# Shifting the start addresses of one group of SBUF tiles (the gated values' parts, and what lies behind them) by 64 and 32 bytes

## The chip, the cores and the metric

The kernel runs on one core of a Trainium2 chip. The metric is the device time of one execution in microseconds. Three executions of the kernel before gave 940.1, 940.12 and 941.05 us, so the median is 940.12 us. Bytes are counted along one of the 128 partitions of SBUF, and the **offset** of a tile is its first byte modulo 256.

## The reference

Masked attention over 8 batches with 8 heads, 576 positions and a head dimension of 64; then, on the 8 × 576 = 4608 tokens with 512 channels, a gated layer of width 1536.

```python
def _attn_ref(q, k, v) -> np.ndarray:
    ...
    scores = scale * np.matmul(q, k.transpose(0, 1, 3, 2))
    mask_local = (rel >= 0) & (rel < stride)
    mask_strided = (rel >= 0) & (pos[None, :] % stride == pos[:, None] % stride)
    ...
    return np.matmul(attn, v).astype(np.float32)

def _moe_ref(x, w_gate, w_val, w_out) -> np.ndarray:
    gate = 1.0 / (1.0 + np.exp(-(x @ w_gate)))
    val = x @ w_val
    return (gate * val @ w_out).astype(np.float32)
```

## The kernel before

**Blocks.** The tokens form nine blocks of 512: block k (0 to 7) holds the first 512 positions of batch k, and block 8 the last 64 positions of all batches. Attention goes batch by batch in four pairs of heads, two with the local mask and two with the strided one. The gated layer goes through 12 slices f of 128 hidden channels each.

**Two parts for each factor.** Matrix products are made of fp32r operands, and each factor is split in two: an upper part (the value rounded to fp32r) and a lower part (the rest). A product is the sum of upper × upper, upper × lower and lower × upper, so every 128x512 product is three matmuls. The inputs' parts are `xh` and `xl`, the weights' parts lie in `w`, and the **parts of the gated value** gate · val are `hh` (upper) and `hl` (lower).

**The gated layer of a block.** Blocks 0, 1 and 2 make gate and value in `products` (L511 to L516): the weights are the stationary operand (128x128), the inputs `xh`, `xl` the moving one (128x512). Blocks 3 to 8 are made two at a time by a scheme with seven products in place of eight (L764 to L780): the products `p` and `d` have weights from a `ring` of tiles as the stationary operand and sums of inputs, `xs`, as the moving one. In all nine blocks `split_high_h` (L534, on ScalarE) rounds the gated value into `hh`, `split_low_h` (L538, on VectorE) writes the rest into `hl`, and `out_products` (L544) multiplies by the output weights: there `hh` or `hl`, 128 columns of it, is the **stationary** operand and the weights `w` the moving one. That makes 9 blocks × 12 slices × 4 pieces × 3 = 1296 matmuls with `hh` or `hl` as the stationary operand. Block 1 makes its gates and values with 12 × 2 × 12 = 288 matmuls, which read `xh1` and `xl1` as the **moving** operand.

**Order.** A table of step names, `ORDER`, is written out by hand; each engine runs its instructions in that order. The first `x` step (upper part of block 0, slice 0) comes some 60 steps ahead of block 0's first output products, while attention of batch 0 is still going.

**Where tiles lie.** Three pools follow each other in SBUF: `keep` (from byte 1152), `work` (from 140,800), and at the end `first`, which is closed when batch 0's second pair is done and gives its room to `odd`. Inside a pool a tag gets its place when it is first used, behind those used before it. `hh` and `hl` have three buffers each and are the last tags of `work`, so what follows in SBUF is only `first`, then `odd`. `first` holds the tiles of batch 0's second pair of heads (its inputs `qk`, `vv` come by DMA). `odd` holds block 1's inputs `xh1`, `xl1`; in the same two places later the plain inputs `xraw` of blocks 3 to 8; and `ost`, from which half of the results and some of the weights' sums are written out. The pad at the end of `cst` (L184) brings the tiles behind it to offset 0:

```python
    wide = SL * KL + GS + P
    cst = pool.tile([P, wide + -(wide + SPARE) % 64], F32, name="cst")[:, :wide]
```

In the kernel before every tile behind `cst` begins at offset 0, and the 128-column pieces of a stationary operand, at multiples of 512 bytes, do so too. `cst` itself begins at offset 128.

Of the kernel before, what the change touches and what calls it, by code (L numbers as in the profile page):

```python
# [9 lines left out]
F32 = mybir.dt.float32  # L10
F32R = mybir.dt.float32r
# [9 lines left out]
P = 128  # L21
# [18 lines left out]
TB = 512  # L40
# [137 lines left out]
def attention_then_glu(ctx, tc, qk_l, qk_s, v_l, v_s, w_all, consts, out):  # L178
    nc = tc.nc
    pool = ctx.enter_context(tc.tile_pool(name="keep", bufs=1))  # L180
    work = ctx.enter_context(tc.tile_pool(name="work", bufs=1))
# [327 lines left out]
    hs = {}  # L509
# [6 lines left out]
            nc.tensor.matmul(o, w, x, start=first and n == 0, stop=last and n == len(todo) - 1)  # L516

    def parts_tiles(k, f):
        hs[k, f] = [work.tile([P, TB], F32R, tag=n, name=f"{n}{k}_{f}", bufs=3) for n in ("hh", "hl")]
        return hs[k, f]  # L520

    def sigmoid(k, f, g):
# [11 lines left out]
    def split_high_h(k, f, by=nc.scalar.copy):  # L534
        hh, _ = parts_tiles(k, f)
        by(hh, whole_h[k, f])  # L536
# [409 lines left out]
```

## Time and profile before

| what | value |
|---|---|
| times of three executions | 940.1, 940.12, 941.05 us; median 940.12 |
| the profiled execution | 940.61 us, of which 938.8 us are the span of its instructions |
| VectorE, ScalarE, GpSimd busy | 604.3, 430.1, 118.1 us |
| waits of TensorE's matmuls that the trace lists | 15.0 us in all, the longest 4.8 us |
| transfers | 154.14 MB, 164 GB/s over the span |

The span runs from the first to the last instruction of the profiled execution. A matmul's row has the time from its start to the modelled end of its last column, 389 ns for a 128x512 one; as they are pipelined, the **pace** (from one start to the next) is shorter, and it is the pace that the engine's time consists of. PE is TensorE's matmul, PEld its loads of stationary operands, which go on beside the matmul ahead; DVE is VectorE, ACT ScalarE, POOL GpSimd, SP the engine that issues most DMAs.

### The profile page before, as it was taken

The page shows a single profiled execution, that of the slowest core. Times are in us where ns is not written, and L with a number is a line of the kernel's source. Part 1 is how long each engine was busy: PE and PEld are TensorE (multiplying, and loading weights), DVE is VectorE, ACT ScalarE, POOL GpSimd, SP SyncE. Part 2 cuts the span into 40 slices and gives each one's busy share as a digit, 9 for nine tenths or more (in the row PEclk, how much of TensorE's full clock was granted, in tenths as well). Part 3 has the DMA queues.
Part 4 walks back from the last instruction along what each step waited for, and adds up shares of the span by engine and source line. Part 5 has one row for each costly group of instructions (what it writes and reads, how often), then busy time and mean ns, then how long its engine had stood idle before and what let it go on. Part 6 is the DMA issues. An engine that isn't in the chain of part 4 may idle for free.

```text
span 938.8 us, 18515 instructions
## 1 busy us (share of the span) xinstructions
PE 919.2 (98%) x7624; PEld 757.2 (81%) x7624; DVE 604.3 (64%) x991; ACT 430.1 (46%) x783; POOL 118.1 (13%) x182
## 2 busy tenths in 40 slices
PE   5999999999999999999999999999999999999998
PEld 4788887888887878888888888888888888888886
DVE  6899766666688998666767897766347433333331
ACT  3899763434364555444445534443434233332221
POOL 0000002544525531000000120000002100000000
PEclk9999999999999999999999999999999999999999
DMA  9773553664656755665555434654444045444111
GB/s 360 264 243 96 166 169 117 190 184 140 201 170 191 226 188 179 212 205 166 179 188 176 156 104 151 213 186 144 146 157 137 21 158 185 150 153 143 64 46 45
DMA packets 90068, 154.14 MB, mean 164 GB/s; under 512 B 5888, under 2 KB 40192, under 8 KB 89984
## 3 DMA queue, kind: packets, MB, share of 16 engines
q1 hardware_dynamic: 89504, 152.31, 50.3%
q8 instruction: 60, 0.98, 0.4%
q10 hardware_dynamic: 480, 0.66, 0.3%
q14 instruction: 24, 0.20, 0.1%
HBM read 121.48 MB, written 31.46 MB: 163 GB/s over the span
## 4 chain that ended last, share of the span: by engine, by line
PE 91%; DVE 4%; DMA 2%; POOL 1%; ACT 1%; issue 1%; SPq 1%; DVEq 0%
PE p L774 21%; PE o L547 19%; PE d L774 16%; PE g L516 9%; PE v L516 8%; PE o_a L547 5%; PE o_g L547 3%; PE o_v L547 3%; PE x_a L437 2%; PE x L437 1%; PE s_g L333 1%; DMA k<-in_qk_s 1%; PE s_v L333 1%; PE s L333 1%; DVE pt L405 1%; PE t L392 1%
## 5 line engine op out<-in xcount | busy, mean ns | idle before, releaser
L774 PE MATMUL p<-xs,ring 128*128 128x512 f32 x864 | 204.6, 389 | 0.0
L774 PEld LDWEIGHTS p<-xs,ring 128*128 128x128 f32 x864 | 162.2, 188 | 33.7
L547 PE MATMUL o<-w,hh 128*128 128x512 f32 x576 | 180.5, 395 | 0.0
L774 PE MATMUL d<-xs,ring 128*128 128x512 f32 x648 | 155.7, 389 | 0.0
L774 PEld LDWEIGHTS d<-xs,ring 128*128 128x128 f32 x648 | 121.6, 188 | 25.3
L547 PEld LDWEIGHTS o<-w,hh 128*128 128x128 f32 x576 | 106.1, 188 | 22.8
L547 PE MATMUL o<-w,hl 128*128 128x512 f32 x288 | 112.1, 389 | 0.0
L808 DVE TENSOR_TENSOR e<-e,d 128x512 f32<-128x512 f32 x54 | 37.1, 687 | 109.2 <-PE d L774 62.1
L405 DVE STREAM_TRANSPOSE pt<-sb 32x320 f32<-32x320 f32 (+1 forms) x192 | 102.9, 536 | 3.8
L516 PE MATMUL g<-xh,w 128*128 128x512 f32 x256 | 86.7, 396 | 2.6 <-DVE sb L353 1.2
L516 PE MATMUL v<-xh,w 128*128 128x512 f32 x256 | 85.4, 391 | 0.0
L803 ACT COPY e<-p 128x512 f32<-128x512 f32 x54 | 31.7, 587 | 117.0 <-PE p L774 116.9
L547 PEld LDWEIGHTS o<-w,hl 128*128 128x128 f32 x288 | 54.1, 188 | 11.5
L516 PEld LDWEIGHTS g<-xh,w 128*128 128x128 f32 x256 | 48.3, 189 | 14.0 <-DVE sb L353 1.8
L516 PEld LDWEIGHTS v<-xh,w 128*128 128x128 f32 x256 | 48.1, 188 | 10.2
L702 POOL TENSOR_TENSOR sum<-sum 128x128 f32<-128x128 f32 x96 | 51.6, 541 | 6.4
L516 PE MATMUL g<-xl,w 128*128 128x512 f32 x128 | 50.1, 392 | 0.0
L540 DVE TENSOR_TENSOR hl<-hid,hh 128x512 fp32r<-128x512 f32 x36 | 28.0, 780 | 34.4 <-ACT hh L536 34.1
L516 PE MATMUL v<-xl,w 128*128 128x512 f32 x128 | 49.8, 389 | 0.0
L816 ACT ACTIVATE e<-e 128x512 f32<-128x512 f32 x54 | 34.2, 633 | 28.7 <-DVE e L808 28.4
L697 POOL TENSOR_TENSOR sum<-w 128x256 f32<-128x256 f32 x44 | 32.5, 759 | 105.3 <-DMA sets<-sum 62.1
L536 ACT CAST hh<-hid 128x512 fp32r<-128x512 f32 x36 | 22.4, 622 | 50.0 <-PE o_a L547 41.2
(140 smaller groups left out, 1381.3 us busy)
## 6 DMA issues: line engine op xcount, KB each, us to landing
ring<-sets SPq DMA_DIRECT2D x126, 512.0 KB, 4.0
raw<-in_w_all SPq DMA_DIRECT2D x36, 512.0 KB, 5.2
vv<-in_v_l SPq DMA_DIRECT2D x15, 640.0 KB, 4.8
qk<-in_qk_s SPq DMA_DIRECT2D x15, 599.0 KB, 5.7
qk<-in_qk_l SPq DMA_DIRECT2D x15, 592.0 KB, 5.0
out<-ob SPq DMA_DIRECT2D x32, 256.0 KB, 2.0
sets<-w SPq DMA_DIRECT2D x24, 256.0 KB, 3.9
sets<-sumh SPq DMA_DIRECT2D x24, 256.0 KB, 2.5
```

The lines of the kernel that those rows point to most:

```text
L333: nc.tensor.matmul(sc[j % len(sc)][g * m : (g + 1) * m, j // len(sc) * BANK + s * kk : j // len(sc) * BANK + (s + 1) * kk], q_[d, at : at ...
L405: nc.vector.transpose(dst[to : to + LB, :, col : col + LB], src[part * LB : (part + 1) * LB, :, h * LB : (h + 1) * LB])
L437: nc.tensor.matmul(at_bank(r, (u * per + g) * m, (u * per + g + 1) * m)[j * D : (j + 1) * D], v[part][rows, slot * P + j * D : slot * P + ...
L516: nc.tensor.matmul(o, w, x, start=first and n == 0, stop=last and n == len(todo) - 1)
L540: by.tensor_tensor(hl, whole_h.pop((k, f)), hh.bitcast(F32), op=ALU.subtract)
L547: nc.tensor.matmul(acc[k][i], h[:, i * P : (i + 1) * P], w, start=f == 0 and n == 0, stop=f == NF - 1 and n == 2,)
L697: nc.gpsimd.tensor_tensor(u[:, at : at + 2], part(wh[f][i], c), part(wl[f][i], c), op=ALU.add)
L702: nc.gpsimd.tensor_tensor(u[:, to], u[:, x], u[:, y], op=op)
L774: nc.tensor.matmul(to, w[:, (wi * 2 + c) * P : (wi * 2 + c + 1) * P], x[xi][:, c], start=p in (1, 2, 5) and c == j == 0, stop=c == 1 and j ...
L803: nc.scalar.copy(x, two[m, 0])
L808: nc.vector.tensor_tensor(x, x, two[m, 1], op=ALU.add)
L816: nc.scalar.activation(x, x, AF.Sigmoid)
```

## The change

When the parts' tiles are asked for the first time (block 0, slice 0), a small tile is placed ahead of each of the two tags, and a memset on GpSimd writes it once:

```diff
     def parts_tiles(k, f):
-        hs[k, f] = [work.tile([P, TB], F32R, tag=n, name=f"{n}{k}_{f}", bufs=3) for n in ("hh", "hl")]
+        hs[k, f] = []
+        for n, ahead in (("hh", 16), ("hl", 56)):
+            if (k, f) == (0, 0):
+                nc.gpsimd.memset(work.tile([P, ahead], F32, tag="gap" + n, name="gap" + n), 0.0)
+            hs[k, f].append(work.tile([P, TB], F32R, tag=n, name=f"{n}{k}_{f}", bufs=3))
         return hs[k, f]
```

The tiles ahead have 64 and 224 bytes. In the two built programs the tiles begin here:

| tiles | byte before | byte now | offset before | offset now |
|---|---|---|---|---|
| all of `keep`, and of `work` ahead of the parts | | the same | 0 | 0 |
| `hh`, first buffer (others 2048 and 4096 further) | 198,144 | 198,208 | 0 | 64 |
| `hl`, first buffer (the same) | 204,288 | 204,576 | 0 | 32 |
| `xh1`, `xraw` (and `sb` of batch 0's second pair) | 210,432 | 210,720 | 0 | 32 |
| `xl1`, `xraw` | 218,624 | 218,912 | 0 | 32 |
| `qk`, `vv` of batch 0's second pair | 213,760, 218,624 | 214,048, 218,912 | 0 | 32 |
| `ost` | 226,816 | 227,104 | 0 | 32 |

The weights `w`, the `ring`, `xs`, and the inputs of blocks 0 and 2 stay at offset 0. So the output products have a stationary operand at offset 64 or 32 against a moving one at 0, block 1's products a stationary one at 0 against a moving one at 32, and all other products both at 0 as before.

On PE, DVE, ACT and SP the instructions, their order and their waits are the same as before. On POOL two are new. This is POOL's program at its start before, from its first memset for the attention (`sb` of batch 0, pairs 1 and 3) to its first sums of weights:

```order
L314 MEMSET sb0_1_81 128x12x10
L314 MEMSET sb0_3_84 128x12x10
L314 MEMSET sb1_1_689 128x12x10
L314 MEMSET sb1_3_1364 128x12x10
L697 ISA
```

And this is the same place now, where the two tiles ahead of the parts have the names gaphh and gaphl:

```order
L314 MEMSET sb0_1_81 128x12x10
L314 MEMSET sb0_3_84 128x12x10
L522 MEMSET gaphh_677 128x16
L522 MEMSET gaphl_680 128x56
L314 MEMSET sb1_1_693 128x12x10
```

The two memsets stand between those of batch 0 and the first of batch 1; they wait for nothing, and nothing waits for them but the memsets behind them on POOL.

## The prediction

> **What bounds the kernel now.** I read the page's head first, then its chain of waits, then stretches of the timeline.
>
> ```profile
> span 938.8 us, 18515 instructions
> PE 919.2 (98%) x7624; PEld 757.2 (81%) x7624; DVE 604.3 (64%) x991; ACT 430.1 (46%) x783; POOL 118.1 (13%) x182
> PE 91%; DVE 4%; DMA 2%; POOL 1%; ACT 1%; issue 1%; SPq 1%; DVEq 0%
> ```
>
> TensorE has 98% of the span and 91% of the chain that ended last. A table of stretches shows how little else there is:
>
> ```profile
> core 0: us, PE busy (x) PEld busy (x) DVE busy (x) ACT busy (x) POOL busy (x), PEclk, DMA share, GB/s
> 0.00:35.00 35.00, 23.62 (x600) 19.58 (x601) 24.76 (x46) 16.02 (x37) 0.54 (x6) 1.00 0.91 341
> 360.00:540.00 180.00, 180.00 (x1586) 148.72 (x1585) 128.96 (x211) 85.32 (x156) 6.40 (x8) 1.00 0.58 185
> 735.00:905.00 170.00, 170.00 (x752) 140.77 (x751) 57.50 (x85) 50.35 (x85) 0.00 (x0) 1.00 0.39 122
> ```
>
> Only the first 35 us have real gaps (11.4 us). From 360 to 540 us and from 735 to 905 us TensorE is busy in every microsecond. So in most of the kernel the time is the number of matmuls times their **pace**, and the change leaves the number as it is. The pace is read from a piece of the chain that holds output products alone:
>
> ```profile
> 714.04 8.16 PE o L547 x36
> 893.55 8.16 PE o L547 x36
> ```
>
> 8.16 / 36 = 0.2267 us, in both stretches. The groups by shape show which matmuls the change can touch:
>
> ```profile
> L774 PE MATMUL p<-xs,ring 128*128 128x512 f32 x864 | 204.6, 389 | 0.0
> L547 PE MATMUL o<-w,hh 128*128 128x512 f32 x576 | 180.5, 395 | 0.0
> L774 PE MATMUL d<-xs,ring 128*128 128x512 f32 x648 | 155.7, 389 | 0.0
> L547 PE MATMUL o<-w,hl 128*128 128x512 f32 x288 | 112.1, 389 | 0.0
> ...
> L547 PE MATMUL o_a<-w,hh 128*128 128x512 f32 x144 | 44.3, 389 | 0.0
> L547 PE MATMUL o_a<-w,hl 128*128 128x512 f32 x72 | 28.0, 389 | 0.0
> L547 PE MATMUL o_g<-w,hh 128*128 128x512 f32 x72 | 22.4, 392 | 0.0
> L547 PE MATMUL o_v<-w,hh 128*128 128x512 f32 x72 | 22.2, 389 | 0.0
> ...
> L547 PE MATMUL o_g<-w,hl 128*128 128x512 f32 x36 | 14.0, 389 | 0.0
> L547 PE MATMUL o_v<-w,hl 128*128 128x512 f32 x36 | 14.0, 389 | 0.0
> ```
>
> The rows of L547 add up to 576 + 288 + 144 + 72 + 72 + 72 + 36 + 36 = 1296 matmuls with `hh` or `hl` as the stationary operand. With block 1's 288 (the moving operand shifts) 1584 matmuls have a shifted operand; the 1512 of L774 have none. One nanosecond of pace on the 1584 is 1.6 us, and 0.2% of the time is 1.9 us, about the least that a measurement of this kernel can tell from no change: a change of pace by 0.0012 us would be seen.
>
> **The change, part by part.**
>
> *The two memsets.* POOL's rows at the start of the timeline:
>
> ```profile
> 0.73 0.34 POOL L314 MEMSET sb<- 128x120 f32 x2 [0.29 <-POOLq L934]
> 45.07 0.21 POOL L314 MEMSET sb<- 128x120 f32 x1 [44.01 <-PE t L396]
> ```
>
> Both stand between these two, where POOL sits idle for 44.01 us. Each writes 16 or 56 columns, fewer than the 120 that take 0.21 us. Cost: at most 0.4 us inside a 44 us hole, so 0. Without that cover they would delay a memset that attention of batch 1 needs, by the same 0.4 us.
>
> *The loads of stationary operands.* A load begins with the matmul ahead of it and goes on beside it:
>
> ```profile
> L547 PEld LDWEIGHTS o<-w,hh 128*128 128x128 f32 x576 | 106.1, 188 | 22.8
> ```
>
> 188 ns of load in a pace of 227 ns leave 22.8 us / 576 = 40 ns. A load from offset 64 or 32 that takes up to a fifth longer stays hidden, if the load's own length is all that matters. I take 0.
>
> *The pace with an operand off 0.* This is the one unknown. No 128x512 matmul of the trace has its operands at different offsets, so it must be bounded. The nearest rows are the strided scores, whose operands walk through SBUF in steps of 216 bytes:
>
> ```profile
> 218.99 0.22 PE L333 MATMUL s_v<-qk 64*64 64x54 f32 x1
> ...
> 219.05 0.22 PE L333 MATMUL s_v<-qk 64*64 64x54 f32 x1
> ...
> 219.11 0.22 PE L333 MATMUL s_v<-qk 64*64 64x54 f32 x1
> ...
> 219.17 0.22 PE L333 MATMUL s_v<-qk 64*64 64x54 f32 x1
> ...
> 219.23 0.22 PE L333 MATMUL s_v<-qk 64*64 64x54 f32 x1
> ```
>
> Each of these rows opens a step of four matmuls; the stationary operand begins at offsets 16, 232, 192 and 152 in the four steps from 219.05 on (and 56 in the one ahead), the moving one 112 bytes further round. Each step takes 0.06 us whatever its offsets. These matmuls are small and may be held back by something else, so that is a sign and no proof. A second sign: `p`, `d`, `o` and `o_a` take 389 ns in the mean, or a little more behind attention, although their tiles lie at many places from 5,632 to 210,000 bytes; what matters can at most be the address below 512. Upper bound of the pace: the slowest start-to-start that the trace shows without a wait, right behind the attention's small matmuls, where load and stream have not yet fallen into step:
>
> ```profile
> 76.78 0.50 PE L516 MATMUL v<-xh,w 128*128 128x512 f32 x1
> 77.12 0.40 PE L516 MATMUL v<-xl,w 128*128 128x512 f32 x1
> 77.36 0.63 PE L516 MATMUL v<-xh,w 128*128 128x512 f32 x2
> ...
> 79.67 0.39 PE L547 MATMUL o<-w,hh 128*128 128x512 f32 x1
> ```
>
> 77.12 to 77.36 is 0.240 us, 0.0133 over the pace: 1584 × 0.0133 = +21 us. Lower bound: at the start TensorE runs at about half its pace (four transposes from 14.69 to 15.73, against 99.78 to 100.31 later: 1.04 / 0.53 = 1.96), and there a 128x512 matmul takes 0.43 us:
>
> ```profile
> 14.69 1.11 PE L392 MATMUL t<-cst,sb 128*128 128x128 f32 x4
> 15.73 0.42 PE L396 MATMUL t<-cst,sb 64*64 64x64 f32 x2
> ...
> 31.79 0.63 PE L516 MATMUL g<-xl,w 128*128 128x512 f32 x1
> 32.22 0.63 PE L516 MATMUL g<-xh,w 128*128 128x512 f32 x1
> ...
> 99.78 0.60 PE L392 MATMUL t<-cst,sb 128*128 128x128 f32 x4
> 100.31 0.30 PE L396 MATMUL t<-cst,sb 64*64 64x64 f32 x2
> ```
>
> 0.43 / 1.96 = 0.219 us; with the rounding, 0.218. So up to 0.0087 us of the full pace are something that half pace hides, and if the shift removed it all: 1584 × 0.0087 = −13.8 us. Between −13.8 and +21 I take 0, since the nearest rows (the scores) show no dependence on the offset.
>
> The Trainium skill, "TensorE: Matmul & The Clock Gate", section "Back-to-back issue gap", gives a matmul of 512 columns 512/2.4 + 2.5 = 215.8 ns from start to start; this trace disagrees, with 226.7. If equal offsets were what costs the 10.9 ns, an estimate by that page's figure is 1584 × 0.0109 = 17.3 us less.
>
> *Writers and readers of the shifted tiles on other engines.*
>
> ```profile
> L540 DVE TENSOR_TENSOR hl<-h,hh 128x512 fp32r<-128x512 f32 x36 | 24.8, 689 | 13.8 <-ACT hh L536 13.8
> L808 DVE TENSOR_TENSOR hid<-hid,d 128x512 f32<-128x512 f32 x36 | 24.8, 688 | 13.2 <-ACT hid L803 12.1
> ```
>
> VectorE needs 689 ns with both inputs in SBUF at offset 0, and 688 with one in PSUM: equal offsets cost it nothing that a shift could give back. If a shift made VectorE, ScalarE or GpSimd slower by a tenth on these tiles, the work stays in stretches in which TensorE is busy throughout (180.00 of 180.00 us above). I take 0; what would come late if that cover went is the next slice's output products, by 0.07 us a slice, 108 slices: 7.5 us.
>
> *Transfers into and out of shifted tiles.* Batch 0's second pair loads its inputs into tiles at offset 32, in the stretch where the queue bounds the start:
>
> ```profile
> q<-in_qk_l SPq DMA_DIRECT2D x1, 288.0 KB, 5.1
> ...
> cst<-in_consts SPq DMA_DIRECT2D x1, 251.0 KB, 4.2
> ```
>
> The constants (second row) go to offset 128 and take 4.2 us for 251 KB (16.7 ns a KB); the queries beside them go to offset 0 and take 5.1 for 288 (17.7). Offset 128 costs nothing, and I take 0 for 32. The two loads, 599 and 384 KB, take 3.0 us at the 341 GB/s of the first 35 us; a tenth more would be 0.3 us.
>
> The Trainium skill, "DMA: Bandwidth & Descriptors", section "How a descriptor splits into AXI transactions", has a descriptor that does not start at a multiple of 256 bytes pay for the bytes back to that multiple, which speaks against the change. For rows of 4,792 bytes an estimate by it is one piece more on 19, some 0.2 us at the start; no run here shows it.
>
> *Sum.* 940.61 us for the profiled execution (span 938.8 and 1.8 around it) plus 0. That execution lies 0.49 above the median of the runs shown, so the forecast is 940.1 us.
>
> **The rivals.**
>
> *Slower: load and stream out of step.* While a matmul streams, the next stationary operand is read from the same memory. Behind each stop the pace is worse for some ten matmuls and then settles: from 77.12 to 79.67 us eleven starts take 2.55 us, 0.2318 each. If operands at different offsets keep them in that unsettled state, the price is 0.0051 × 1584 = 8.1 us: **948.2 us**. For it: the settled pace is reached only with both operands at 0. Against: the scores' steps. It decides from 0.0012 us a matmul on.
>
> *Faster: equal offsets are what collides.* If the excess over half pace (0.0087 us) is the two reads meeting at equal offsets, all of it may go: **926.3 us**. For it: at half pace it is absent. Against: a stream of 2,048 bytes runs through every offset eight times, so the start's offset should matter little; and the scores again.
>
> *Same, for a reason of its own:* the pace is that of the moving stream alone and no address enters. That is the forecast.
>
> That the change doesn't do what it says is out: the tiles' bytes in the built program are those of the table.
>
> **How the numbers follow.** No change 0.58, slower 0.24, faster 0.18: the scores' steps and the one pace at all places carry the first; the missing row keeps the others alive, and the settling behind stops gives the slower one a little more. The likeliest case alone has 938.6 to 941.8. To leave out no more than 2 in 10 the range goes on to either side: down to 932, over about half of the faster cases (six tenths of the −13.8), and up to 950, past 948.2, over most of the slower ones; the bounds of 926 and 961 are left out as tails.
>
> **What would show it.** Right: the rows of L547 keep 389 ns, both 36-matmul pieces keep 8.16 us, and PE keeps 919 us busy. Slower rival: those rows at 394 or so and the pieces at 8.3, while L774 keeps 389. Faster rival: the pieces near 7.85. If block 1 alone changed (between 140 and 241 us), the moving operand's offset is what counts, and not the stationary one's. A later first strided score would show the transfers, and idle time of PE ahead of L547 the writers.

## The result and the profile after

| | before | after |
|---|---|---|
| median of three executions | 940.12 us | 947.24 us (946.25 to 947.95) |
| ratio to before, 95% interval | | 1.0072, 1.0049 to 1.0094 |
| the profiled execution, its span | 940.61, 938.8 us | 947.24, 945.4 us |

The changed kernel is 7.1 us slower; the interval of the ratio makes that 4.6 to 8.8 us. The head of the page after, with the span and the engines' busy time:

```profile
span 945.4 us, 18517 instructions
PE 926.1 (98%) x7624; PEld 756.7 (80%) x7624; DVE 606.4 (64%) x991; ACT 431.0 (46%) x783; POOL 117.6 (12%) x184
```

The same 7624 matmuls keep TensorE busy for 926.1 us where they took 919.2: 6.9 us more, and the span is 6.6 us longer. The idle time ahead of the matmuls' groups adds up to 14.7 us, before to 15.2. So it isn't waits that grew; matmuls themselves come slower. Which ones, the groups by shape of the changed kernel say (L547 is now L551, L774 is L778; the last figures of a row are busy us, mean ns of one, idle time):

```profile
L778 PE MATMUL p<-xs,ring 128*128 128x512 f32 x864 | 204.6, 389 | 0.0
L551 PE MATMUL o<-w,hh 128*128 128x512 f32 x576 | 183.7, 400 | 0.0
L778 PE MATMUL d<-xs,ring 128*128 128x512 f32 x648 | 155.6, 389 | 0.0
L551 PE MATMUL o<-w,hl 128*128 128x512 f32 x288 | 112.6, 391 | 0.0
...
L551 PE MATMUL o_a<-w,hh 128*128 128x512 f32 x144 | 45.4, 396 | 0.0
L551 PE MATMUL o_a<-w,hl 128*128 128x512 f32 x72 | 28.1, 390 | 0.0
L551 PE MATMUL o_g<-w,hh 128*128 128x512 f32 x72 | 22.9, 399 | 0.0
L551 PE MATMUL o_v<-w,hh 128*128 128x512 f32 x72 | 22.7, 396 | 0.0
...
L551 PE MATMUL o_v<-w,hl 128*128 128x512 f32 x36 | 14.0, 390 | 0.0
L551 PE MATMUL o_g<-w,hl 128*128 128x512 f32 x36 | 14.0, 390 | 0.0
```

Two things are to be seen. The products at L778, whose operands the change did not move, have the durations of before to the nanosecond. The eight rows of the output products are longer: they add up to 443.4 us of busy time, where those of before add up to 437.5. The rows of neighbours overlap, so the time lost is read from the pace, which the chain of waits after shows (start us, length us, what):

```profile
718.52 8.32 PE o L551 x36
...
899.33 8.32 PE o L551 x36
```

8.32 / 36 = 0.2311 us a matmul, where before it was 0.2267; both pieces of 36 lost the same 0.16 us. The 1296 output products are 36 such pieces: 5.8 us. Each 128-column piece is a triple of matmuls, two with `hh` and one with `hl`, and inside a triple the starts of the trace show an uneven beat: 236 ns from the first upper part to the second, 232 from the second to the lower one, 226 from the lower one to the next triple (median of each).

The other matmuls with a moved operand are block 1's gates and values. Their groups by shape between 140.5 and 241 us, after:

```profile
L516 PE MATMUL v<-xh,w 128*128 128x512 f32 x88 | 29.4, 395 | 0.0
...
L516 PE MATMUL v<-xl,w 128*128 128x512 f32 x44 | 17.4, 395 | 0.0
```

and the same window before:

```profile
L516 PE MATMUL v<-xh,w 128*128 128x512 f32 x88 | 28.9, 389 | 0.0
...
L516 PE MATMUL v<-xl,w 128*128 128x512 f32 x44 | 17.1, 389 | 0.0
```

Here each matmul's row is 6 ns longer. By the starts, from the thirteenth of a run on, the pace is 233.3 ns where before it was 226.7: 6.6 ns more, on 288 matmuls 1.9 us. With the 5.8 us of the output products that is 7.7 us, inside the interval of 4.6 to 8.8. The span of the profiled execution grew by 6.6 us only; executions of one and the same kernel differ by as much as the rest (before: 938.3 to 941.3 us in all).

Of the other terms that the prediction priced at nothing, none shows a cost. POOL's start and the writers of the parts, after:

```profile
0.73 0.33 POOL L314 MEMSET sb<- 128x120 f32 x2 [0.29 <-POOLq L938]
1.00 0.11 POOL L522 MEMSET gaphh<- 128x16 f32 x1
1.05 0.14 POOL L522 MEMSET gaphl<- 128x56 f32 x1
43.88 0.20 POOL L314 MEMSET sb<- 128x120 f32 x1 [42.68 <-PE t L396]
```

```profile
L544 DVE TENSOR_TENSOR hl<-h,hh 128x512 fp32r<-128x512 f32 x36 | 24.8, 688 | 13.8 <-ACT hh L540 13.8
```

```profile
L551 PEld LDWEIGHTS o<-w,hh 128*128 128x128 f32 x576 | 106.2, 188 | 24.0
```

The two memsets lie in POOL's hole of 42.7 us. VectorE needs 688 ns for a lower part at offset 32, where it needed 689. A load from offset 64 is recorded with the same 188 ns as one from offset 0: **the loads are not recorded as longer, the matmuls only start further apart**. The first strided score of the pair whose inputs were shifted starts at 8.96 us, before at 9.01, so the transfers brought nothing late.

### The profile page after: what moved, and what is told of

Same layout as the page of the kernel before. It is cut to its first block, busy times and chain, and to the rows that moved or that the text cites. A ratio compares the mean times of both kernels' runs of the same rounds, so it can differ in the third digit from the quotient of the medians.

```text
span 945.4 us, 18517 instructions
## 1 busy us (share of the span) xinstructions
PE 926.1 (98%) x7624; PEld 756.7 (80%) x7624; DVE 606.4 (64%) x991; ACT 431.0 (46%) x783; POOL 117.6 (12%) x184
## 4 chain that ended last, share of the span: by engine, by line
PE 91%; DVE 4%; DMA 2%; POOL 1%; ACT 1%; SPq 1%; issue 1%; DVEq 0%
PE p L778 21%; PE o L551 20%; PE d L778 16%; PE g L516 9%; PE v L516 9%; PE o_a L551 5%; PE o_g L551 3%; PE o_v L551 3%; PE x_a L437 2%; PE x L437 1%; DMA k<-in_qk_s 1%; PE s_g L333 1%; PE s_v L333 1%; DVE pt L405 1%; PE t L392 1%; PE s L333 1%
## 5 line engine op out<-in xcount | busy, mean ns | idle before, releaser
L778 PE MATMUL p<-xs,ring 128*128 128x512 f32 x864 | 204.6, 389 | 0.0
L778 PEld LDWEIGHTS p<-xs,ring 128*128 128x128 f32 x864 | 162.2, 188 | 33.8
L551 PE MATMUL o<-w,hh 128*128 128x512 f32 x576 | 183.7, 400 | 0.0
L778 PE MATMUL d<-xs,ring 128*128 128x512 f32 x648 | 155.6, 389 | 0.0
L778 PEld LDWEIGHTS d<-xs,ring 128*128 128x128 f32 x648 | 121.7, 188 | 25.2
L551 PEld LDWEIGHTS o<-w,hh 128*128 128x128 f32 x576 | 106.2, 188 | 24.0
L551 PE MATMUL o<-w,hl 128*128 128x512 f32 x288 | 112.6, 391 | 0.0
L551 PEld LDWEIGHTS o<-w,hl 128*128 128x128 f32 x288 | 54.1, 188 | 13.3
```

The costliest lines, as they stand in the source:

```text
L551: nc.tensor.matmul(acc[k][i], h[:, i * P : (i + 1) * P], w, start=f == 0 and n == 0, stop=f == NF - 1 and n == 2,)
L778: nc.tensor.matmul(to, w[:, (wi * 2 + c) * P : (wi * 2 + c + 1) * P], x[xi][:, c], start=p in (1, 2, 5) and c == j == 0, stop=c == 1 and j ...
```

## The experiments

Three theories were open after the result.

- **Distance**: a matmul's pace depends on how far apart its two operands begin, modulo some number of bytes.
- **Own offset**: an operand that does not begin at a multiple of 256 bytes is read more slowly, whatever the other does.
- **Neither**: the tiles' places in SBUF as such, the memsets, or the second pair's transfers.

The times of before beside which each run is set were taken along with it on the same chip: 940.15 us (19 executions) for the first three kernels, 939.63 (11) for the two with both parts at one offset, 940.34 (12) for the last. The three kernels of bare matmuls were executed once each; from their second series on TensorE's granted clock is 1.00.

**Only the parts moved.** The padding goes on to the next multiple of 256 behind the parts, so that block 1's inputs and all else stay at offset 0:

```diff
-        hs[k, f] = [work.tile([P, TB], F32R, tag=n, name=f"{n}{k}_{f}", bufs=3) for n in ("hh", "hl")]
+        both = {}
+        for n, ahead in (("hl", 8), ("hh", 8), ("end", 48)):
+            if (k, f) == (0, 0):
+                nc.gpsimd.memset(work.tile([P, ahead], F32, tag="gap" + n, name="gap" + n), 0.0)
+            if n != "end":
+                both[n] = work.tile([P, TB], F32R, tag=n, name=f"{n}{k}_{f}", bufs=3)
+        hs[k, f] = [both["hh"], both["hl"]]
```

> hh at offset 64 and hl at 32 as in the change, everything behind them back at offset 0 modulo 256. Both theories have TensorE's pace as the cause: three output matmuls took 0.694 us in the change's trace against 0.680 before, 432 times 0.0140 is 6.0 us, so 946.1 us. If the pace of the output products depended on what lies behind the parts as well, or the loss came from block 1 and the transfers alone, the time would be under 943.

Measured: 945.8 us (944.13 to 947.0), +5.65, ratio 1.0060 (1.0045 to 1.0075). The chain of waits of this kernel:

```profile
717.08 8.32 PE o L553 x36
```

The output products have the same 8.32 us as with the whole change. The order of the two tags was turned round here and made no difference.

**Only what lies behind the parts moved.** The other half alone:

```diff
+        if (k, f) == (0, 0):
+            nc.gpsimd.memset(work.tile([P, 8], F32, tag="gapend", name="gapend"), 0.0)
```

> hh and hl back at offset 0, only the tiles behind them (block 1's inputs, moving operands) at 32. By the pace of the change's trace (0.2335 against 0.2267 us on 288 matmuls) 2.0 us more than before: 942.1 us. If a shifted moving operand costs nothing by itself: 940.1.

Measured: 942.2 us (941.08 to 943.46), +2.05, ratio 1.0024 (1.0015 to 1.0034). The chain, and a row of block 1's products between 140.5 and 241 us:

```profile
714.64 8.16 PE o L549 x36
```

```profile
L516 PE MATMUL v<-xh,w 128*128 128x512 f32 x88 | 29.4, 395 | 0.0
```

The output products are back at 8.16, block 1's keep their 395 ns. So a moved moving operand costs time as a moved stationary one does, and the two parts together (5.65 + 2.05 = 7.7 us) give the change's 7.1 within its interval.

**Everything moved together.** All tiles behind the constants begin at offset 64, so that every 128x512 matmul has both operands there:

```diff
-    cst = pool.tile([P, wide + -(wide + SPARE) % 64], F32, name="cst")[:, :wide]
+    cst = pool.tile([P, wide + -(wide + SPARE) % 64 + 16], F32, name="cst")[:, :wide]
```

> Every tile behind the constants moves by 64 bytes, so that both operands of every 128x512 matmul begin at offset 64. Theory of the distance (the load of the next stationary operand and the stream of the moving one are read together, and only the distance of their offsets counts): no change, 940.1 us, and 0.2267 us a matmul. Rival, each operand's own offset counts (a start off a multiple of 256 bytes costs an access of its own): all 3672 matmuls lose some 0.005 to 0.009 us, 18 to 33 us more, 958 to 973.

Measured: 940.74 us (939.15 to 941.23), ratio 1.0002 (0.9992 to 1.0011), with the pieces at before's length:

```profile
714.39 8.16 PE o L547 x36
```

This is the run that decides: an offset of 64 costs nothing that shows (-0.8 to +1.0 us by the interval) as long as both operands have it. The own-offset theory, which wanted a loss in every product, falls.

**The pace by itself.** A kernel of matmuls alone, in series of 36. `m` is the moving operand's offset in bytes, `s` the stationary one's, and the pieces step by 2048 and 512 bytes as in the kernel:

```python
...
for i in range(N):
    a, b = m // 4 + 512 * (i % 2), ss[i % len(ss)] // 4 + 128 * (i % 4)
    nc.tensor.matmul(o, w[:, b : b + P], x[:, a : a + 512], start=i == 0, stop=i == N - 1)
...
```

> Only matmuls: a series of 36 of 128x512 for each pair of offsets m (moving) and s (stationary) in bytes, after two series at 0 and 0; nothing of the reference is computed. A series at 0 and 0 takes 36 times 0.2267, 8.16 us. Distance theory: the series with m equal to s take 8.16 too, and those with the same difference take the same time as each other (m32s0, m64s32, m96s64, m128s96 alike; m0s32, m32s64, m64s96, m96s128 alike), 8.2 to 8.6. Own-offset theory: the time of a pair is a cost of m plus a cost of s, so m64s64 is slower than m64s0 and m0s64. In both the series with 64, 64, 288 in turn takes 12 times 0.694, 8.33 us, and the period is 256 or 512 bytes (m0s256 like m0s0, or not).

The timeline of it, a row for each series (start us, length us):

```profile
25.67 8.55 PE L43 MATMUL m0s32x<-x,w 128*128 128x512 f32 x36
34.06 8.56 PE L43 MATMUL m0s64x<-x,w 128*128 128x512 f32 x36
...
67.65 8.40 PE L43 MATMUL m0s192x<-x,w 128*128 128x512 f32 x36
75.89 8.56 PE L43 MATMUL m0s224x<-x,w 128*128 128x512 f32 x36
84.28 8.33 PE L43 MATMUL m0s256x<-x,w 128*128 128x512 f32 x36
92.45 8.55 PE L43 MATMUL m0s288x<-x,w 128*128 128x512 f32 x36
...
376.94 8.36 PE L43 MATMUL m64s64x<-x,w 128*128 128x512 f32 x36
385.13 8.36 PE L43 MATMUL m96s96x<-x,w 128*128 128x512 f32 x36
...
426.12 8.55 PE L43 MATMUL m32s64x<-x,w 128*128 128x512 f32 x36
434.51 8.55 PE L43 MATMUL m64s96x<-x,w 128*128 128x512 f32 x36
```

From the start of one series to that of the next, over 36: m0s32 8.39 / 36 = 0.2331 us, m0s256 0.2269, m0s192 0.2289, m64s64 0.2275, m32s64 0.2331. A series needs some matmuls to settle behind the one ahead; from the thirteenth on the mean is sharper:

```
distance s - m modulo 256       pace, ns
0   (m = s at 0, 32, 64, 96, 128, 192, 256 or 288; m0s256; m256s0)   226.7
192 (m0s192, m0s448, m64s0, m320s0)                                 228.8
32, 64, 96, 128, 160, 224       232.7 to 234.6
```

At multiples of 32, which are all that the 128x512 matmuls of these kernels have, the distance theory holds: the pace has a period of 256 bytes in the distance, and m32s64, m64s96 and m96s128 have that of m0s32 (233.4). The series m32s0, which has block 1's offsets in the changed kernel, has 233.3, as block 1 has there. Below 32 the distance isn't all: m16s16 has 229.9 ns, though its operands are level; that was not expected. A second expectation missed. The series with the kernel's own three offsets (64, 64, 288 against 0) has 235.6 ns, where the kernel has 231.1. By 235.6 the output products would lose 11.5 us, twice the 5.65 measured. The kernel takes its pieces in another order (it uses each piece of `hh` twice running), so the pace of a mixed sequence depends on more than the distance of each matmul's operands; which part of the order does it wasn't tested.

**The distances back in the kernel.** Both parts go to one offset, first 64, then 192, and what lies behind returns to 0. For 64 (for 192 the two numbers are exchanged):

```diff
+        if (k, f) == (0, 0):
+            nc.gpsimd.memset(work.tile([P, 16], F32, tag="gap", name="gap"), 0.0)
         hs[k, f] = [work.tile([P, TB], F32R, tag=n, name=f"{n}{k}_{f}", bufs=3) for n in ("hh", "hl")]
+        if (k, f) == (0, 0):
+            nc.gpsimd.memset(work.tile([P, 48], F32, tag="gapend", name="gapend"), 0.0)
```

> hh and hl both at offset 64, the rest at 0. By the first probe's series (0.2334 against 0.2267 for a stationary operand at 64 beside a stream at 0) 1296 times 0.0068 is 8.8 us: 948.9 us, more than with 64 and 32, where the three loads in turn gave 0.694 a triple (6.0 us). If offsets matter only where they change from one operand to the next, 940.

> The same with both parts at offset 192, where the first probe has 0.2288 us a matmul: 1296 times 0.0021 is 2.7 us, 942.9 us. If any offset off 0 costs the same in the kernel, 948.9.

Measured: 948.28 us at 64 (946.76 to 949.75), +8.65, ratio 1.0094 (1.0076 to 1.0112); 942.41 us at 192 (940.93 to 943.42), +2.78, ratio 1.0027 (1.0016 to 1.0038). The chain at 64:

```profile
716.90 8.40 PE o L551 x36
```

and at 192:

```profile
714.77 8.24 PE o L551 x36
```

8.40 / 36 = 0.2333 and 8.24 / 36 = 0.2289 us: the paces of the two series of the kernel of matmuls alone. So for both kernels that table forecasts the added time (8.8 and 2.7 us) within 0.2 us of the medians, with intervals of 7.1 to 10.5 and 1.5 to 3.6 us, as long as both parts have one offset. They also show that the loss doesn't grow with the shift: 192 costs a third of 64.

**Finer steps.** Is there a distance with a better pace than 226.7? Series of 32 with the stationary operand at 4, 8, … 252 bytes and the moving one at 0, in the same loop.

> Only matmuls: 32 of 128x512 for each offset s of the stationary operand from 4 to 252 in steps of 4, the moving one at 0. By the first probe: 7.25 us a series (0.2267 a matmul) at distance 0, 7.32 at 192, 7.47 (0.2334) at the other multiples of 32. Distance theory in its simple form, in which distance 0 is the best: no series under 7.25. Rival: 0 is only one of several good distances, and some multiple of 4 gives less than 0.2267, down to 0.2133 (512 columns at the pace of the attention's row in the text); then a version faster than both kernels is to be had.

```profile
202.52 7.42 PE L36 MATMUL m0s100x<-x,w 128*128 128x512 f32 x32
209.78 7.62 PE L36 MATMUL m0s104x<-x,w 128*128 128x512 f32 x32
...
320.78 7.74 PE L36 MATMUL m0s164x<-x,w 128*128 128x512 f32 x32
328.36 7.62 PE L36 MATMUL m0s168x<-x,w 128*128 128x512 f32 x32
...
484.48 7.42 PE L36 MATMUL m0s252x<-x,w 128*128 128x512 f32 x32
491.73 7.43 PE L36 MATMUL m0s0x<-x,w 128*128 128x512 f32 x32
```

From start to start over 32, in us: 0.2269 at 100, 0.2369 at 164, 0.2266 at 252. From the thirteenth matmul on, 226.7 ns stands at 0, 100, 120, 132, 144, 156, 228 and 252, and everything else lies between 228.3 and 237.8 in no order that the rows show. None of the 64 distances is below 226.6. So with the moving operand at 0 nothing better than 226.7 was found, and that is the pace of the kernel before; the 0.2133 us that the rival hoped for is not reached.

**Which operations it takes.** Series of 48 with other shapes and types at distances 0, 32, 128 and 192, and series that alternate between two pairs of offsets.

```python
PAIRS = [(0, 0), (0, 32), (0, 128), (0, 192)]
...
SERIES += [("r", c, 512, (p,)) for c in (128, 64, 32) for p in PAIRS]
SERIES += [("r", 128, n, (p,)) for n in (256, 128) for p in PAIRS]
SERIES += [("b", 128, 512, (p,)) for p in PAIRS]
SERIES += [("r", 128, 512, p) for p in (((0, 0), (32, 32)), ((0, 32), (32, 0)), ((0, 0), (128, 128)), ((0, 128), (128, 0)))]
...
```

> Only matmuls, 48 a series. First, what meets what. If the load of the next stationary operand disturbs the stream that runs beside it, the series with the pairs 0,0 and 32,32 in turn is slow (0.233; stream at 0 beside a load at 32) and the one with 0,32 and 32,0 in turn is fast (0.2267; stream 0 beside load 0). If a matmul's own two operands count, the other way round. Second, where the loss sits. If it arises during the load, it is the same in ns with 256 columns of stream (some 120 ns at distance 0, 127 at 32) and halves with 64 columns of stationary operand (some 220 and 223); if it belongs to the stream's own columns it halves with the stream and stays with the load. bf16 reads half the bytes: less loss or none.

The timeline (r is fp32r, b bf16, the first number the columns of the load, n those of the stream):

```profile
193.11 5.52 PE L46 MATMUL r128n128m0s32x<-x,w 128*128 128x128 f32 x48
...
198.47 5.52 PE L46 MATMUL r128n128m0s128x<-x,w 128*128 128x128 f32 x48
...
209.19 10.53 PE L46 MATMUL b128n512m0s0x<-xb,wb 128*128 128x512 bf16 x48
219.56 10.52 PE L46 MATMUL b128n512m0s32x<-xb,wb 128*128 128x512 bf16 x48
229.92 10.52 PE L46 MATMUL b128n512m0s128x<-xb,wb 128*128 128x512 bf16 x48
```

The means from the thirteenth matmul on, in ns:

```
distance                           0       32      128     192
fp32r, load 128, stream 512     226.8   233.4   232.4   228.9
fp32r, load  64, stream 512     229.8   231.6   229.3   228.4
fp32r, load  32, stream 512     231.6   240.1   230.4   231.7
fp32r, load 128, stream 256     120.0   118.3   118.7   117.8
fp32r, load 128, stream 128     111.7   111.7   111.7   111.7
bf16,  load 128, stream 512     215.9   215.9   215.9   215.9
alternating (m, s): (0,0) (32,32) 231.7; (0,32) (32,0) 233.5; (0,0) (128,128) 228.4; (0,128) (128,0) 230.0
```

The bf16 rows start 10.36 us apart whatever the distance: of the two types tried, only fp32r shows the effect. A stream of 128 columns shows nothing of it, with 111.7 ns at every distance. The simple pictures missed: the loss doesn't shrink with the columns of the load, it doesn't halve with the stream (with 256 columns the distance 0 is the slowest), and of the alternating series neither the one that keeps each matmul's own operands at distance 0, (0,0) (32,32), nor the one that keeps the next load at distance 0 to the stream beside it, (0,32) (32,0), has the 226.7. Which operand disturbs which is therefore not settled; among these series only the ones in which every matmul stands alike, at distance 0, have the good pace.

**A shift by 256 bytes.** A control for the third theory: one memset and a tile of 256 bytes ahead, so that the parts, block 1's inputs and all behind them move but keep offset 0.

```diff
+        if (k, f) == (0, 0):
+            nc.gpsimd.memset(work.tile([P, 64], F32, tag="gap", name="gap"), 0.0)
         hs[k, f] = [work.tile([P, TB], F32R, tag=n, name=f"{n}{k}_{f}", bufs=3) for n in ("hh", "hl")]
```

> One memset and one tile of 256 bytes ahead of hh: hh, hl, xh1, xl1, xraw and ost all move by 256 bytes and keep the offset 0. Distance theory (only the distance of the two operands' starts modulo 256 counts): 940.1 us, and the pieces of 36 output products at 8.16. Rival (the memset, or the place of the parts and of the odd pool's tiles in SBUF, has a share in the loss): later by that share, up to the 7.1 us of the change.

Measured: 939.49 us (938.54 to 940.8), ratio 0.9994 (0.9984 to 1.0003).

```profile
713.82 8.16 PE o L549 x36
```

Neither the memset nor the place in SBUF has a share in the loss that shows (-1.5 to +0.3 us by the interval). What is left is how far apart the two operands begin, modulo 256.

No version was faster than before, and no distance tried has a better pace than the 226.7 ns that the kernel before has already.

## Why the prediction was wrong

*The step that failed* is the last sentence on the pace: "Between −13.8 and +21 I take 0, since the nearest rows (the scores) show no dependence on the offset." The runs showed 4.4 ns a matmul in its place on the 1296 output products and 6.6 ns on block 1's 288. The scores could not have shown that, for two reasons. First, both of their operands move on by the same 216 bytes from step to step: "the moving one 112 bytes further round" means that the distance is one and the same in all the steps. They varied only the common shift, and the kernel with everything at 64 shows that a common shift costs the 128x512 matmuls nothing. Second, they are plain fp32 matmuls of 54 columns that come 15 ns apart (0.06 us for four), and rows of another shape need not show what an address costs. The series with 128 columns is a case of that kind: 111.7 ns at every distance, while the same load with 512 columns loses 6.6 ns at 32. What paces the scores wasn't tested. The prediction had seen the second danger ("may be held back by something else") but not the first, and still let those rows decide.

*The second sign* was read the wrong way. One pace at many places from 5,632 to 210,000 bytes was put down to places not mattering, with the remark that "what matters can at most be the address below 512". All these places are multiples of 256, so the distance was 0 in every one: the trace held no information on any other. The settling rows behind the attention's small matmuls, at 0.2318, were what the trace had of this shape at a slower pace without a wait.

*The slower rival* had the place and the condition: operands at different offsets. That its size came out too, 0.2318 us a matmul, read from the settling behind a stop, against 0.2311 in the output products and 0.2333 in block 1, 8.1 us against 7.1 measured, is in part luck: both parts at 192 would have cost 2.78 us and both at 64 8.65, and by the rival's one price (0.0051 × 1296) either costs 6.6. Whether a run at other distances is the same state as the settling behind a stop, no run shows. Its "against" was the scores' steps, which fell. Its signs came as it gave them: rows of L551 at 390 to 400 ns, pieces at 8.32, L778 still at 389. The forecast's same-for-a-reason case ("the pace is that of the moving stream alone and no address enters") falls with the run in which only the parts moved. The upper bound was not the slowest row that it was said to be (76.78 to 77.12, shown beside it, is 0.34 us), but every series of 128x512 matmuls with a full load lies under its 0.240.

*The faster rival* is out: unequal offsets made the matmuls slower, and none of 64 distances beats 0. So no shift tried gives back the excess of the kernel's pace over the 0.218 us read at half pace. The excess is absent with bf16: 215.9 ns against 226.7 in the same loop. The Trainium skill, "TensorE: Matmul & The Clock Gate", section "Back-to-back issue gap", has 215.8 ns for 512 columns as the gap of a single matmul by itself, and 131 ns for a stream of loads and matmuls. The bf16 series, which is such a stream, agrees with the first figure and not with the second, and no fp32r series here comes down to either.

*The terms at nothing* were right: memsets in POOL's hole, loads of 188 ns, VectorE's 688 ns. Of the transfers into shifted tiles, the kernel with only the tiles behind the parts moved bounds the cost: of its 2.05 us (1.4 to 3.2) block 1's products account for 1.9. The prediction's estimate of one piece more on 19 for rows of 4,792 bytes is a slip: from offset 32 they reach into 19 pieces of 256 bytes, as from offset 0. Nothing hung on it.

*What stays open* is the mechanism below the distance: why a run of fp32r matmuls that stand alike settles at 226.7 ns for some distances and in a longer beat (226, 232, 236 in a triple) for most. The runs say that fp32r shows it and bf16 doesn't, that at multiples of 32 bytes both operands' addresses enter by their difference modulo 256, and that neighbours in the sequence matter. How the reads are arranged below that, no run here shows.

## What to carry to other kernels

In a stretch where TensorE is busy throughout with fp32r products, check the start of both operands modulo 256 bytes, and keep the difference at 0: pads of 64 and 224 bytes ahead of two tags cost 0.7% here without any new wait or longer row on another engine. When a trace shows one value for everything, first ask whether the thing in question varied at all in it: here the scores varied two offsets and never their distance. Rows of another shape count only if they are bound by the same thing. What no row shows can be measured with a kernel of bare series: where both parts had one offset, its table gave the added time to 0.2 us; where they had two, the series in another order was out by a factor of two.

## What the runs showed of the hardware

- fp32r 128x512 matmuls, each with a load of its own, start 226.7 ns apart when the two operands' first bytes lie at multiples of 32 and differ by a multiple of 256, and 228.3 to 237.8 at most other distances. At multiples of 32 the distance alone counts, and not the two addresses (m = s at each multiple tried is as good as 0): pairs of one distance agree to 0.8 ns within a kernel of series, and m0s128 has 232.4, 232.8 and 233.6 in the three of them. Below that it doesn't: m at 4 against s at 0 has 236.6, m at 0 against s at 252 has 226.7, with the same distance.
- With the moving operand at 0 there are good places for the stationary one that are no round numbers (100, 120, 132, 144, 156, 228, 252), and the worst, 164, stands between ordinary ones.
- bf16 matmuls of the same shape start 215.9 ns apart at each of the four distances tried.
- The Trainium skill, "SBUF — State Buffer", section "Who interferes with whom", has TensorE's ports for the moving operand and for loads independent of each other. The bf16 series have nothing against it at four distances. With fp32r the pace changes by up to 11 ns a matmul with the distance of the two operands, although no load is recorded as longer, so there the two are not independent of each other.
